# Another order of work inside each segment of a memory-recurrent attention kernel: value projections later, transposes in pairs, softmax in two queue entries

## The chip, the cores and the metric

The kernel runs on one core of a Trainium2 chip. The core has a matrix engine (PE; its weight loads are listed as PEld), a vector engine (DVE), a scalar engine (ACT), a general engine (POOL) and a sync engine (SP), which here only issues transfers. Sixteen DMA engines move data between HBM and the on-chip memory. Each engine takes its own list of instructions strictly in order, and a semaphore wait at the head of a list holds up everything behind it. The metric is the device time in microseconds (us); lower is better.

## The reference, cut to what matters

The sequence of 2048 tokens with 640 features is worked through in 64 segments of 32 tokens. Eight memory rows are carried from one segment to the next, so a segment can't start before the one before it has ended.

```python
for s in range(n_seg):                       # 64, one after the other
    h = concat([mem, x[:, 32*s:32*s+32]])    # 8 memory rows + 32 tokens = 40 rows
    q = einsum('btd,dhe->bhte', h, Wq)       # 32 heads of 192
    k = einsum('btd,dhe->bhte', h, Wk)
    v = einsum('btd,dhe->bhte', h, Wv)
    p = softmax(where(mask, q @ k.T * 192**-0.5, -1e9))
    o = einsum('bhte,hed->btd', p @ v, Wo)
    mem = o[:, :8]                           # into the next segment
    outs.append(o[:, 8:])
b   = (gelu(x @ w_gate) * (x @ w_up)) @ w_down
g   = sigmoid((x * gate_w).sum(-1, keepdims=True))
out = g * concat(outs) + (1 - g) * b
```

## The kernel before, in words

A first stage computes the whole feed-forward branch `b` and stores it in HBM. A second stage (the left stage, lines 795 to 823) computes the projections of Q and K for those eight tokens of each segment whose values don't depend on the memory, for all segments at once, and stores them in HBM ("left stores", four DMAs for each group of heads, issued by ACT). The third stage is the chain of 64 segments, and it takes most of the time. Four segments make a group of 128 rows; in the text q0 to q3 are the first to the fourth segment of such a group. A q0 segment does twice the matmuls in its value projections, since it also does the memory-free rows of V for the whole group (`left` in `v_oct`), and it finishes the output of the previous group (`out_group`, `out_store`).

Inside a segment the 32 heads are taken as four octets of eight heads, numbered 0 to 3. `PROG` (line 464) is the order of the work, written out by hand: a list of items such as `("q", 1)`. `segment` (line 1025) walks through it and hands each operation to `_Sched.add`, which appends it to its engine's list and finds out which earlier operations it has to wait for. So the order of `PROG` is the order of every engine's queue.

- `q` and `k` (`cmode`, L871): the projection of one octet, five weight pieces with four matmuls each, into one bank of PSUM. Then `rows_evac` (ACT, L877) copies the bank to the row buffer `rows_sb` in on-chip memory. There is one such buffer, so the copy for K is queued behind the transposes of Q.
- `tq` and `tk` (`row_transp`): three PE transposes (L883) of the row buffer, and the evacuation into `Qs` on DVE (L887) or into `Ks` on ACT (L890, L894).
- `v` (`v_oct`, L905): as `q`, evacuated by ACT (L916) into one of two buffers; in q0 a second bank is evacuated by DVE (L919).
- `sc` (`scores`): a mask matmul (L926) and 16 score matmuls (L937) into bank 5 or 6 (octet even or odd), then the whole softmax: maximum (L952) and subtraction (L954) on DVE, exponential on ACT (L956), sum (L958), reciprocal (L960) and two products (L962, L963) on DVE. It also queues the POOL copies of the left columns for the next octet (L835, L839).
- `pt` (`p_transp`): two PE transposes of the probabilities (L971, L972) into the same bank 5 or 6, spread by two DVE products (L974, L977) into `PTm` and `PTl`.
- `pv` (`pv_oct`): six matmuls (L991, L993) and the evacuation into `uT` by ACT (L1001) and DVE (L1005, L1007).
- `wo` (`wo_part`, L1020): the output projection of an octet in six pieces of ten matmuls each, summed in bank 7 over the whole segment. For octet 2 it is split into three parts. At the end ACT (L1070) writes the memory rows of the next segment.

All other banks come in turn from `misc_bank` (five banks).

Not all weights fit in on-chip memory. The planner (lines 480 to 509) adds up the `COST` entries along `PROG` for a due time of every weight piece, and picks the pieces to be streamed so that they are evenly spaced in time, as many as memory needs: 24 of the 84 pieces. The others stay resident. A streamed piece goes through a ring of five slots: SP issues the DMA for a piece (L549) as soon as the piece that was five places earlier has been read by PE. In the first segment SP also loads 22 resident pieces (`load_late`, L597) whose memory the left stage held until then, each some 24 pieces ahead of its use and in one queue with the ring.

## Time and profile before

| what | value |
|---|---|
| median of 3 runs | 2227.48 us (2223.69 to 2227.95) |
| the profiled execution | span 2220.5 us; 7.0 us less than the median run, as the span goes from the first instruction to the last only; the page gives no other time of it |
| PE busy | 1912.3 us (86%) |
| DVE, ACT, POOL busy | 943.6 (42%), 799.7 (36%), 273.6 us (12%) |
| moved by DMA | 642.75 MB, 601.01 MB of it by SP's queue |
| left stage ends, chain begins | about 292 us |
| first segment ends | 353.7 us |
| last segment begins | 2185.9 us |

A line such as "L871 PE MATMUL ps<-arena ... x9762 | 465.2, 330 | 61.6 <-DMA ... 20.0" says: 9,762 matmuls from line 871 kept PE busy for 465.2 us, 330 ns each by the record (they overlap); before them PE was idle for 61.6 us in all, 20.0 of it until a DMA landed. "arena" is the on-chip memory and "ps" the PSUM. A row of the view by windows gives a stretch, its length, the busy time of each engine with the number of instructions, the granted clock of TensorE (1.00 is full), the share of time for which the DMA engines were busy, and GB/s. This share can be over 1 for a short window, as packets overlap.

### The profile page before, as it was taken

Reading aid. Unit: us, or ns where it says so; the run is one execution under the profiler, and the core shown is the slowest. Engines: PE = TensorE matmul, PEld = TensorE weight load, DVE = VectorE, ACT = ScalarE, POOL = GpSimd, SP = SyncE. Lnnn points to the kernel's source line nnn. Section 1 sums busy time; section 2 is a strip of 40 time slices with the busy share of each in tenths; the row PEclk is TensorE's granted clock in tenths of the full one; section 3 lists DMA queues with packets and bytes.
Section 4 is the critical chain, followed back from the end, with each engine's and each line's share of the span. In section 5 each row is a group of like instructions: output and inputs, shape, how many; then the busy total and the mean of one; then the engine's idle time right before and its main releaser. Section 6 shows DMA issues by size and latency. Waiting matters only on the chain.

```text
span 2220.5 us, 94985 instructions
## 1 busy us (share of the span) xinstructions
PE 1912.3 (86%) x41834; PEld 1231.3 (55%) x41862; DVE 943.6 (42%) x3184; ACT 799.7 (36%) x2248; POOL 273.6 (12%) x1210
## 2 busy tenths in 40 slices
PE   7999958888888888888888888888888888888887
PEld 3544425555555555555565655555555655555655
DVE  2222223444444444444444444444444544444444
ACT  2222223334333333343333333333333334333333
POOL 0000001111111111111111111111111111111111
PEclk9999989999999999999999999999999999999999
DMA  9203579999999999999999999999999999999998
GB/s 370 88 13 112 150 236 331 322 303 316 301 318 307 324 303 311 305 316 312 319 320 311 316 300 320 306 313 310 320 302 321 309 322 311 315 315 316 310 309 278
DMA packets 363257, 642.75 MB, mean 289 GB/s; under 512 B 60498, under 2 KB 231770, under 8 KB 362842
## 3 DMA queue, kind: packets, MB, share of 16 engines
q1 hardware_dynamic: 311770, 601.01, 80.2%
q10 hardware_dynamic: 51072, 35.66, 5.4%
q8 instruction: 327, 5.36, 0.9%
q14 instruction: 88, 0.72, 0.1%
HBM read 618.74 MB, written 17.83 MB: 287 GB/s over the span
## 4 chain that ended last, share of the span: by engine, by line
PE 46%; DMA 32%; DVE 14%; ACT 3%; issue 3%; ACTq 2%; SPq 0%; DVEq 0%
PE ps L871 12%; DMA arena<-in_A_Wv_dram 10%; DMA arena<-in_A_Wo_dram 9%; PE ps L1020 9%; DMA arena<-in_A_Wk_dram 8%; PE ps L905 7%; DMA arena<-in_A_Wq_dram 4%; DVE arena L974 4%; PE ps L804 3%; PE ps L883 2%; PE ps L742 2%; PE ps L739 2%; ACTq L819 2%; PE ps L757 2%; DVE ps L954 2%
## 5 line engine op out<-in xcount | busy, mean ns | idle before, releaser
L871 PE MATMUL ps<-arena 128*32 128x384 bf16 x10240 | 488.1, 330 | 69.6 <-DMA arena<-in_A_Wk_dram 23.6
L1020 PE MATMUL ps<-arena 128*128 128x40 bf16 x15360 | 457.9, 180 | 64.8 <-DVE arena L1007 38.1
L1020 PEld LDWEIGHTS ps<-arena 128*128 128x128 bf16 x15360 | 428.9, 96 | 88.8 <-DVE arena L1007 49.5
L871 PEld LDWEIGHTS ps<-arena 128*32 128x32 bf16 x10240 | 247.1, 97 | 254.6 <-DMA arena<-in_A_Wk_dram 63.2
L905 PE MATMUL ps<-arena 128*32 128x384 bf16 x6400 | 324.4, 331 | 53.3 <-DMA arena<-in_A_Wv_dram 30.2
L877 ACT ACTIVATE arena<-ps 128x384 bf16<-128x384 f32 x512 | 249.8, 488 | 181.0 <-PE ps L871 105.1
L974 DVE TENSOR_TENSOR arena<-ps,arena 128x320 bf16<-128x320 bf16 x256 | 125.8, 491 | 387.0 <-PE ps L972 387.0
L835 POOL COPY arena<-arena 128x96 bf16<-128x96 bf16 x256 | 67.4, 263 | 1665.0 <-PE ps L937 1138.3
L956 ACT ACTIVATE ps<-ps 104x160 f32<-104x160 f32 x256 | 71.9, 281 | 494.5 <-DVE ps L954 494.5
L905 PEld LDWEIGHTS ps<-arena 128*32 128x32 bf16 x6400 | 144.6, 96 | 175.5 <-DMA arena<-in_A_Wv_dram 59.2
L883 PE MATMUL ps<-arena 128*128 128x128 bf16 x1536 | 175.9, 223 | 32.0 <-ACT arena L877 31.9
L1001 ACT ACTIVATE arena<-ps 128x320 bf16<-128x320 f32 x256 | 112.3, 439 | 215.4 <-PE ps L993 213.8
L991 PE MATMUL ps<-arena 128*128 128x160 bf16 (+1 forms) x768 | 130.5, 260 | 57.1 <-DVE arena L977 39.6
L916 ACT ACTIVATE arena<-ps 128x384 bf16<-128x384 f32 x256 | 125.6, 491 | 139.0 <-PE ps L905 138.7
L839 POOL COPY arena<-arena 64x32 bf16<-64x32 bf16 (+1 forms) x768 | 165.4, 215 | 47.3
L883 PEld LDWEIGHTS ps<-arena 128*128 128x128 bf16 x1536 | 88.1, 98 | 135.7 <-ACT arena L877 91.1
L952 DVE TENSOR_REDUCE arena<-ps 104x4 f32<-104x160 f32 x256 | 80.9, 316 | 149.3 <-PE ps L937 149.3
L894 ACT ACTIVATE arena<-ps 64x128 bf16<-64x128 bf16 x512 | 136.8, 267 | 6.3
L887 DVE COPY arena<-ps 128x384 bf16<-128x384 bf16 x256 | 89.4, 349 | 102.0 <-PE ps L883 102.0
L993 PE MATMUL ps<-arena 128*128 128x64 bf16 (+1 forms) x768 | 124.5, 202 | 4.0 <-ACT arena L877 4.0
L958 DVE TENSOR_REDUCE arena<-ps 104x4 f32<-104x160 f32 x256 | 83.1, 325 | 99.8 <-ACT ps L956 99.8
L991 PEld LDWEIGHTS ps<-arena 128*128 128x128 bf16 x768 | 72.3, 97 | 91.2 <-DVE arena L977 90.7
(81 smaller groups left out, 1886.3 us busy)
## 6 DMA issues: line engine op xcount, KB each, us to landing
arena<-in_A_Wo_dram SPq DMA_DIRECT2D x591, 320.0 KB, 4.7
arena<-in_A_Wv_dram SPq DMA_DIRECT2D x398, 384.0 KB, 5.2
arena<-in_A_Wk_dram SPq DMA_DIRECT2D x340, 384.0 KB, 5.3
arena<-in_A_Wq_dram SPq DMA_DIRECT2D x276, 384.0 KB, 5.0
left_qk_scratch<-arena ACTq DMA_DIRECT2D x16, 768.0 KB, 8.7
arena<-left_qk_scratch ACTq DMA_DIRECT2D x64, 192.0 KB, 4.6
arena<-in_A_x_dram SPq DMA_DIRECT2D x4, 640.0 KB, 15.0
ffn_b_scratch<-arena ACTq DMA_DIRECT2D x16, 160.0 KB, 1.8
```

The source lines that it names most:

```text
L839: S_.add("pool", lambda e, a=a, b=b, lo=lo, hi=hi, sa=sa: e.tensor_copy(out=Ks[lo:hi, a:b, L:R], in_=stg[lo:hi, o, 1, sa:sa + b - a]), rea ...
L871: S_.add("pe", [lambda e, j=j, k=k, g_=g_: e.matmul(ps[32 * j:32 * j + 32, bank, 0:384], Hb[hb][:, k, 0:L], g_[:, 384 * j:384 * (j + 1)], ...
L877: S_.add("act", lambda e: e.activation(out=rows_sb, in_=ps[:, bank, 0:384], func=ACTF.Copy), reads=[r_ps[bank]], writes=[r_rows], name="ro ...
L883: S_.add("pe", [lambda e, c=c: e.transpose(pv[:, c * 128:(c + 1) * 128], rows_sb[:, c * 128:(c + 1) * 128], ident) for c in range(3)], rea ...
L894: S_.add("act", lambda e, a=a, lo=lo: e.activation(out=Ks[lo:lo + 64, a:a + 4, 0:L], in_=src[lo:lo + 64, 1], func=ACTF.Copy), reads=[r_ps[ ...
L905: return [lambda e, j=j: e.matmul(ps[32 * j:32 * j + 32, bk, 0:384], lhs, g_[:, 384 * j:384 * (j + 1)], start=(k == 0), stop=(k == KT - 1) ...
L916: S_.add("act", lambda e: e.activation(out=v_sb[o % NVB], in_=ps[:, bank, 0:384], func=ACTF.Copy), reads=[r_ps[bank]], writes=[r_v[o % NVB ...
L974: S_.add("dve", lambda e: e.tensor_tensor(out=PTm, in0=apx(pv[:, 512:616], [[64, 2], [0, 4], [1, R]]), in1=apx(mbd, [[0, 2], [1, 4], [0, R]]),
L991: return [lambda e: e.matmul(full, v[:, e0:e0 + 128], PTm[:, ia:ib], start=True, stop=False, skip_group_check=True), lambda e: e.matmul(pa ...
L993: lambda e: e.matmul(part, vl[:, e0:e0 + 128], PTl[:, ia:ib], start=False, stop=True, skip_group_check=True)]
L1001: S_.add("act", lambda e: e.activation(out=apx(u[:, 0, 0, :], [[2 * R, 2], [3 * R, 4], [1, R]]), in_=ps[:, A, 0:2 * W].rearrange("p (c t r ...
L1020: fns.append(lambda e, g_=g_, i=i, c=c, n=n, tl=tl, cc=cc, u=u: e.matmul(ps[:, OB, n * R:(n + 1) * R], g_[:, i, n * 128:(n + 1) * 128], u[ ...
```

## The change

The operations of a segment are the same, and their numbers too; the order in which the queues get them is another.

- `PROG` is rewritten. The value projections stand before the transposes (octets 0 and 1), or far behind (`v` 2 behind `pt` 1, `v` 3 behind `pt` 3); `tq` and `tk` always follow each other; `pt` and `pv` of an octet have other work between them.
- There are two row buffers, one for Q and one for K. `rows_evac` for K is queued directly behind its projection.
- `scores` ends with the subtraction. Exponential, sum, reciprocal and products are a function of their own, `probs`, queued by a new item `sm`.
- The extra work that hung on `k` (output of the previous group, transposes of x, copies, gate) now hangs on `tk`.
- The second row buffer takes 768 bytes of each partition from the resident weights, and the `COST` entries are others (`sc` 0.5, `pv` 0.45, `wo` 0.26, `tq` and `tk` 0.25, `sm` 0).

```diff
-    wsB["rows"] = al(768)
+    wsB["rows"] = al(2 * 768)
...
-    PROG = [("q", 0), ("k", 0), ("tq", 0), ("v", 0), ("tk", 0),
-            ("q", 1), ("k", 1), ("sc", 0), ("tq", 1), ("v", 1), ("tk", 1),
-            ("q", 2), ("k", 2), ("pt", 0), ("sc", 1), ("tq", 2), ("pv", 0), ("v", 2), ("tk", 2),
-            ("q", 3), ("k", 3), ("pt", 1), ("sc", 2), ("tq", 3), ("pv", 1), ("v", 3), ("tk", 3),
-            ("wo", 0), ("pt", 2), ("sc", 3), ("pv", 2), ("wo", 1), ("wo", 2, 0), ("pt", 3), ("wo", 2, 1), ("pv", 3),
-            ("wo", 2, 2), ("wo", 3)]
+    PROG = [("q", 0), ("k", 0), ("v", 0), ("tq", 0), ("tk", 0),
+            ("q", 1), ("k", 1), ("v", 1), ("sc", 0), ("tq", 1), ("tk", 1), ("sm", 0),
+            ("q", 2), ("k", 2), ("sc", 1), ("tq", 2), ("tk", 2), ("pt", 0), ("sm", 1),
+            ("q", 3), ("k", 3), ("sc", 2), ("pv", 0), ("tq", 3), ("tk", 3), ("pt", 1), ("sm", 2),
+            ("v", 2), ("sc", 3), ("wo", 0), ("pv", 1), ("pt", 2), ("sm", 3),
+            ("wo", 1), ("pv", 2), ("pt", 3), ("v", 3),
+            ("wo", 2, 0), ("wo", 2, 1), ("pv", 3), ("wo", 2, 2), ("wo", 3)]
...
-    COST = dict(q=0.17, k=0.17, v=0.2, sc=0.6, pt=0.2, pv=0.5, wo=0.27, tq=0.2, tk=0.2)
+    COST = dict(q=0.17, k=0.17, v=0.2, sc=0.5, sm=0.0, pt=0.2, pv=0.45, wo=0.26, tq=0.25, tk=0.25)
...
-    def rows_evac(bank):
-        S_.add("act", lambda e: e.activation(out=rows_sb, in_=ps[:, bank, 0:384], func=ACTF.Copy),
-               reads=[r_ps[bank]], writes=[r_rows], name="rows evac")
+    def rows_evac(m, bank):
+        S_.add("act", lambda e: e.activation(out=rows_sb[m], in_=ps[:, bank, 0:384], func=ACTF.Copy),
+               reads=[r_ps[bank]], writes=[r_rows[m]], name="rows evac")
...
         S_.add("dve", lambda e: e.tensor_tensor(out=S3, in0=S3, in1=mxb, op=ALU.subtract),
                reads=[rb, rst], writes=[rb], name="smax sub")
+
+    def probs(s, o):
...
         S_.add("act", lambda e: e.activation(out=S3, in_=S3, func=ACTF.Exp, bias=0.0, scale=scale),
                reads=[rb], writes=[rb], name="smax exp")
...
             if kind in ("q", "k"):
-                qkbank[kind] = misc_bank()
-                cmode(s, "qk".index(kind), i, qkbank[kind])
-                if kind == "q":
-                    rows_evac(qkbank["q"])
-                if kind == "k" and i == 0 and q == 0 and g > 0:
+                m = "qk".index(kind)
+                bank = misc_bank()
+                cmode(s, m, i, bank)
+                rows_evac(m, bank)
+            elif kind == "tq":
+                row_transp(s, 0, i)
+            elif kind == "tk":
+                row_transp(s, 1, i)
+                if i == 0 and q == 0 and g > 0:
                     out_group(g - 1, misc_bank())
...
-            elif kind == "tq":
-                row_transp(s, 0, i)
-                rows_evac(qkbank["k"])
-            elif kind == "tk":
-                row_transp(s, 1, i)
+            elif kind == "sm":
+                probs(s, i)
```

More of the change, by code (lines that the diff above doesn't have):

```diff
@@ L383, in _build @@
     r_Kz = [sreg(o_K + 8 * R * 2, 4 * R * 2, 64, 128), sreg(o_K + 12 * R * 2, 4 * R * 2, 0, 64)]
-    rows_sb = bview(wsB_off["rows"], 768)
-    r_rows = sreg(wsB_off["rows"], 768)
+    rows_sb = [bview(wsB_off["rows"] + b * 768, 768) for b in range(2)]
+    r_rows = [sreg(wsB_off["rows"] + b * 768, 768) for b in range(2)]
     stg = bview(wsB_off["stg"], NOCT * 2 * LW * 2).rearrange("p (o m c i) -> p o m c i", m=2, c=12, i=M)
@@ L882, in row_transp @@
         pv = psb(bank)
-        S_.add("pe", [lambda e, c=c: e.transpose(pv[:, c * 128:(c + 1) * 128], rows_sb[:, c * 128:(c + 1) * 128], ident)
-                      for c in range(3)], reads=[r_rows, r_ident], writes=[r_ps[bank]], name="T%s s%d o%d" % ("qk"[m], s, o))
+        S_.add("pe", [lambda e, c=c: e.transpose(pv[:, c * 128:(c + 1) * 128], rows_sb[m][:, c * 128:(c + 1) * 128], ident)
+                      for c in range(3)], reads=[r_rows[m], r_ident], writes=[r_ps[bank]], name="T%s s%d o%d" % ("qk"[m], s, o))
         src = pv[:, 0:384].rearrange("p (c t r) -> p c t r", t=4, r=L)
@@ L955, in scores @@
                reads=[rb, rst], writes=[rb], name="smax sub")
+    def probs(s, o):
+        bank = 5 + o % 2
+        S3 = ps[0:104, bank, 0:4 * R].rearrange("p (t r) -> p t r", r=R)
+        mxs, sms, rcs = [x[0:104, :] for x in st_f[o % 2]]
+        rst = r_st[o % 2]
+        rcb = rcs.rearrange("p (t o) -> p t o", o=1).broadcast_to([104, 4, R])
+        rb = r_ps[bank]
         S_.add("act", lambda e: e.activation(out=S3, in_=S3, func=ACTF.Exp, bias=0.0, scale=scale),
@@ L1026, in segment @@
         g, q = s // 4, s % 4
-        qkbank = {}
         for item in PROG:
@@ L1043, in segment @@
                         x_group_transposes(g + 1, misc_bank())
-                if kind == "k" and i == 2:
+                if i == 2:
                     if s + 1 < NSEG:
```

3 lines of the change are left out of this document (1 added, 2 removed).

## The prediction

> **What bounds the kernel now.** I read the page first, then the view by windows, then groups and waits of PE.
>
> ```profile
> span 2220.5 us, 94985 instructions
> ```
>
> The page's shares mix three stages over this span. So I cut the chain at the end of each memory copy (L1070) and asked for 61 of its segments: all at once, then each class q0 to q3 in its turn (last row, and the sum over its segments: 15, 15, 16, 15).
>
> ```profile
> 381.62:2185.94 1804.32, 1560.68 (x38513) 1048.73 (x38513) 822.97 (x2911) 690.62 (x2028) 254.44 (x1128) 0.99 0.93 313
> ...
> 1980.25:2010.76 30.51, 27.73 (x693) 18.89 (x693) 15.82 (x52) 11.44 (x33) 4.08 (x18) 1.00 0.90 302
> sum 463.79, PE 417.23 PEld 283.20 DVE 237.54 ACT 171.69 POOL 61.19; mean PE 27.82 PEld 18.88 DVE 15.84 ACT 11.45 POOL 4.08
> ...
> 2010.76:2040.17 29.41, 24.79 (x608) 16.33 (x608) 12.59 (x46) 11.18 (x33) 4.08 (x18) 1.00 0.95 319
> sum 442.70, PE 375.66 PEld 247.90 DVE 188.95 ACT 168.44 POOL 61.18; mean PE 25.04 PEld 16.53 DVE 12.60 ACT 11.23 POOL 4.08
> ...
> 1922.21:1950.86 28.65, 24.47 (x608) 16.50 (x608) 12.60 (x46) 11.17 (x33) 4.08 (x18) 1.00 0.94 321
> sum 453.79, PE 391.00 PEld 263.30 DVE 201.57 ACT 179.00 POOL 65.25; mean PE 24.44 PEld 16.46 DVE 12.60 ACT 11.19 POOL 4.08
> ...
> 1950.86:1980.25 29.39, 24.95 (x618) 16.68 (x618) 12.99 (x47) 11.44 (x34) 4.46 (x20) 1.00 0.96 316
> sum 444.04, PE 376.79 PEld 254.33 DVE 194.92 ACT 171.50 POOL 66.83; mean PE 25.12 PEld 16.96 DVE 12.99 ACT 11.43 POOL 4.46
> ```
>
> The last three columns are the granted clock, the DMA share and GB/s. A q0 segment takes 463.79 / 15 = 30.9 us with PE busy for 27.8 and DMA for 0.90 of it. The others take 29.5, 28.4 and 29.6 us with PE busy for 25.0, 24.4 and 25.1 and DMA at 0.94 to 0.96. The waits of PE in one q0 segment (first fence) and in the q1 after it (second) show why:
>
> ```profile
> PE ps L905 <- ACT arena L877: 0.9, 2, 0.5
> PE ps L1020 <- DVE arena L1007: 0.8, 2, 0.5
> PE ps L991 <- DVE arena L977: 0.7, 2, 0.4
> PE ps L871 <- ACT arena L1070: 0.3, 1, 0.3
> ```
>
> ```profile
> PE ps L1020 <- DMA arena<-in_A_Wo_dram: 0.7, 2, 0.4
> PE ps L871 <- DMA arena<-in_A_Wq_dram: 0.6, 1, 0.6
> PE ps L1020 <- DVE arena L1007: 0.6, 2, 0.4
> PE ps L991 <- DVE arena L977: 0.4, 1, 0.4
> ...
> PE ps L871 <- DMA arena<-in_A_Wk_dram: 0.4, 1, 0.4
> ```
>
> In q0 PE waits for no DMA: PE and its engine waits set the pace. In the others it waits for weights as well. How full the ring is follows from the issues:
>
> ```profile
> arena<-in_A_Wo_dram SPq DMA_DIRECT2D x591, 320.0 KB, 4.7
> arena<-in_A_Wv_dram SPq DMA_DIRECT2D x398, 384.0 KB, 5.2
> arena<-in_A_Wk_dram SPq DMA_DIRECT2D x340, 384.0 KB, 5.3
> arena<-in_A_Wq_dram SPq DMA_DIRECT2D x276, 384.0 KB, 5.0
> ```
>
> A piece is on its way for about 5.0 us, and 24 of them come in 29.6 us, so 4.1 of five slots are in flight on average. The ring can hardly ask for more. **Segments q1 to q3 are bound by the stream, q0 by PE.** This decides what a PE wait is worth: nearly all in q0, little elsewhere.
>
> **The change part by part.** The waits of PE in the same 61 segments:
>
> ```profile
> L1020 PE MATMUL ps<-arena 128*128 128x40 bf16 x14640 | 436.7, 180 | 62.0 <-DVE arena L1007 36.2 <-DMA arena<-in_A_Wo_dram 22.4 <-issue 1.7
> L905 PE MATMUL ps<-arena 128*32 128x384 bf16 x6080 | 305.7, 329 | 49.8 <-DMA arena<-in_A_Wv_dram 27.0 <-ACT arena L877 21.4 <-issue 0.2
> L883 PE MATMUL ps<-arena 128*128 128x128 bf16 x1464 | 167.2, 223 | 11.8 <-ACT arena L877 11.7
> L991 PE MATMUL ps<-arena 128*128 128x160 bf16 x732 | 124.1, 259 | 54.6 <-DVE arena L977 37.8
> L993 PE MATMUL ps<-arena 128*128 128x64 bf16 x732 | 118.5, 202 | 4.0 <-ACT arena L877 4.0
> ```
>
> *Second row buffer, softmax in two parts.* The K copy now follows its own projection, and the exponential is queued behind the K evacuations. Before, the order of ACT put the exponential first:
>
> ```profile
> 1047.01 0.28 ACT L956 ACTIVATE ps<-ps 104x160 f32<-104x160 f32 x1 [1.90 <-DVE ps L954]
> 1047.21 0.48 ACT L877 ACTIVATE arena<-ps 128x384 bf16<-128x384 f32 x1
> ...
> 1047.74 1.65 PE L905 MATMUL ps<-arena 128*32 128x384 bf16 x36 [0.47 <-ACT arena L877]
> ```
>
> The copy stood behind an exponential that waited for DVE, and the value matmuls, which in q0 take K's bank next, waited 0.47 us for it, twice a segment. All waits on L877 go (21.4 + 11.7 + 4.0 = 37.1 us): 0.9 in a q0, and (37.1 - 15 x 0.9) / 46 = 0.5 in another. New: for octets 2 and 3 a score group now stands where a value projection stood. For octet 2 a copy of 0.48 us and its start against `sc` and `tq` leaves about 0.2 us of wait at `tk`; nothing at the lower bound, 0.5 (the whole copy) at the upper.
>
> *`pt` and `pv` apart.* The 54.6 us before L991 go, 0.9 a segment: behind each `pt` there is now a `wo`, or `q`, `k` and `sc`, 1.8 us (436.7 / 244 for a `wo`) and more against the 0.77 us of L974 and L977 together. If DVE were late by more than 1 us, that cover would be gone.
>
> *New waits in the second half.* The two DVE products, and how `wo` follows `pv` now:
>
> ```profile
> L974 DVE TENSOR_TENSOR arena<-ps,arena 128x320 bf16<-128x320 bf16 x256 | 125.8, 491 | 387.0 <-PE ps L972 387.0
> ...
> L977 DVE TENSOR_TENSOR arena<-ps,arena 128x128 bf16<-128x128 bf16 x256 | 71.7, 280 | 0.0
> ...
> 1062.53 0.69 PE L1020 MATMUL ps<-arena 128*128 128x40 bf16 x20
> 1063.46 1.67 PE L1020 MATMUL ps<-arena 128*128 128x40 bf16 x60 [0.24 <-DVE arena L1007]
> ```
>
> Before, 20 matmuls lie between `pv` 3 and the `wo` that reads its result, and 0.24 us are left; the evacuation takes 0.93 us. `wo` 1 now stands behind `pv` 1 with only the two transposes of `pt` 2 between: a wait of about 0.7 us. The one in front of `wo` (2,0), 0.35 on average (36.2 / 61 less 0.24), goes, as `v` 3 and `pt` 3 lie there. So +0.35; the ends are 0 and 0.7. `sc` 3 writes bank 6, which `pt` 1 used just before; only `v` 2 (305.7 / 304 = 1.0 us) covers, while DVE has to finish the maximum of `sc` 2, `uT`, Q and both products. I take 0.4 us in q1 to q3, none in q0 where `v` 2 is twice as long; the ends are 0 and 0.77.
>
> So PE's own need falls by 0.9 + 0.9 - 0.35 - 0.2 = 1.25 us in q0, and by 0.5 + 0.9 - 0.35 - 0.2 - 0.4 = 0.45 in the others.
>
> *What is streamed.* The planner's arithmetic, redone with the new `PROG`, `COST` and 768 bytes less, gives 24 pieces again, but 8 of Wo, 6 of V, 5 of K and 5 of Q where 9, 6, 5 and 4 stood: one piece of 320 KB became one of 384. Its price is 64 KB at the queue's own rate:
>
> ```profile
> q1 hardware_dynamic: 311770, 601.01, 80.2%
> ```
>
> 0.802 x 2220.5 us for 601 MB makes 0.19 us for 64 KB (65,536 bytes). By the landing times it is less: 0.5 us more (4.7 against 5.2) with 4.1 in flight makes 0.12. I take 0.12, since small and large pieces share the same queue and the difference of landing is measured there; at a share of about 0.945 (the rows of q1 to q3 show 0.94 to 0.96) that is 0.13 us a segment where the stream binds. The ends are 0 and 0.2. The spacing is as even as before: with each item at its PE time, five streamed pieces in a row span 4.5 to 6.1 us before and 4.5 to 6.4 after.
>
> *Moved extras, POOL and SP.* `out_group`, the x transposes and the gate move by one value projection and two transposes; their results are needed a segment later. POOL's left copies still have the two projections in front of the next `sc`. All at nothing; POOL is busy for 4.1 of 29.6 us a segment.
>
> *First segment, once.* ACT sits in the issue of the left stores and the load behind them, with Q's copy queued behind:
>
> ```profile
> 313.46 0.50 PE L883 MATMUL ps<-arena 128*128 128x128 bf16 x3 [19.64 <-ACT arena L877]
> ...
> 312.00:316.00 4.00, 2.54 (x31) 1.32 (x35) 0.36 (x1) 0.98 (x2) 0.14 (x1) 0.50 0.87 213
> 316.00:320.00 4.00, 4.00 (x71) 1.81 (x65) 0.56 (x1) 2.16 (x6) 0.77 (x4) 0.68 0.56 165
> ```
>
> Now `v` 0 runs before that wait and frees a slot, so SP gets further down its list of late loads. The idle DMA time of the two windows, 0.13 x 4 + 0.44 x 4 = 2.3 us, is what this can win. I take 2, with ends of -4 and +2. Of the clock the row shows 0.50 after the wait. The Trainium skill (TensorE: Matmul & The Clock Gate, What's actually happening) says that an idle window of about 3.4 us halves the clock; this row agrees, and by that rule `v` 0 in the shadow wins only its full-clock time, as what follows starts cold instead.
>
> *The sum.* In q0 the stream needs 0.90 x 30.9 + 0.12 = 27.9 us, at the share of 0.945 of the others 29.6; PE needs 30.9 - 1.25 = 29.7. Two needs that near to each other are not met in step: I take 29.9, so -1.0 us, 15 times: -15. In the 48 others: +0.13 x 48 = +6.2, and PE, ready 0.45 us earlier, keeps the ring fuller; from a share of 0.945 to 0.948, inside what the rows show, is 0.1 us, so -4.8. The first segment: -2. In all 15.6 less than the profiled execution's span of 2220.5; that span lies 7.0 below the median of the runs, which I keep: 2227.5 - 15.6 = 2212 us.
>
> **The rivals.**
>
> *A: the stream has room.* Then PE's gain counts everywhere: 15 x 1.25 + 46 x 0.45 = 39, so with the first segment 2186. For it: with many transfers waiting the engines do more:
>
> ```profile
> 300.00:304.00 4.00, 0.00 (x0) 0.00 (x0) 0.00 (x0) 0.00 (x0) 0.00 (x0) 0.50 1.05 402
> ```
>
> Against it: there the queue was deep, here it is five slots, 4.1 of them used. The Trainium skill says to judge DMA by HBM use, not by the engines' busy share (Perfetto Trace Analysis, Identifying the Most-Contended Engine), and gives about 358 GB/s a core (DMA: Bandwidth & Descriptors, Specifications); 313 is 87% of it, so by that rule A holds. The 402 GB/s of this row disagree with the limit.
>
> *B: the waits only move.* The new waits stand at their upper ends: `wo` 1 at 0.7, `sc` 3 at 0.77, `tk` at 0.5. In q1 to q3 PE then loses 1.97 - 1.4 = 0.57 us, which fits into its DMA waits (0.7 + 0.6 + 0.4 = 1.7 us in the q1 shown); in q0 1.8 - 1.2 = 0.6 is left, 9 us in all, and the larger piece takes 6.2 of it: about 2225, no change. For it: `pv` 1 and its reader are neighbours now.
>
> *C, slower: the stream binds q0 too.* If its share stays at 0.90 there, with or without PE's waits, only the larger piece is left: 64 x 0.13 to 64 x 0.2 = 8 to 13 us, so 2236 to 2240. It decides once the new DMA waits of PE in a q0 segment pass 1.25 us. For it: a ring of five can't work ahead into q0. Against it: not one DMA wait in the q0 rows above.
>
> **How the numbers follow.** The forecast has 0.48 (its own range 2197 to 2222), A 0.16, B 0.13, C 0.23. Faster, the same, slower: 0.64, 0.13, 0.23; the runs shown lie within 0.2%, which is about what can be told from no change. The range, 2180 to 2237, leaves out the outer part of A and of C.
>
> **What would show it.** Right: no wait on the row copies in q0 segments; those near 29.9 us with DMA waits; q1 to q3 unchanged within 0.3 us with DMA at 0.95; a wait of 0.7 us in front of `wo` 1. Wrong: a DMA share of 0.97 or more with q1 to q3 below 28.7 us (A), or a q0 still near 30.9 us (C).

## The result, and the profile after

The changed kernel takes 2204.35 us (median of 4 runs, 2201.96 to 2208.51); the kernel before takes 2225.64 us beside it (4 runs, 2223.69 to 2227.95). The ratio is 0.9914, with a 95% interval of 0.9894 to 0.9933: 0.9% faster, 21 us by the medians. The profiled execution took 2205.25 us, with a span of 2203.5 us.

The same cut at the memory copies (L1078 now) gives the view by windows of the kernel after: the whole of the 61 segments, then the sums over the 15, 15, 16 and 15 segments of q0 to q3.

```profile
383.10:2168.30 1785.20, 1524.01 (x38513) 1049.37 (x38513) 825.10 (x2911) 734.43 (x2028) 254.50 (x1128) 0.98 0.95 318
...
sum 447.00, PE 402.65 PEld 283.46 DVE 236.65 ACT 180.16 POOL 61.19; mean PE 26.84 PEld 18.90 DVE 15.78 ACT 12.01 POOL 4.08
...
sum 440.00, PE 363.37 PEld 247.01 DVE 190.06 ACT 179.96 POOL 61.20; mean PE 24.22 PEld 16.47 DVE 12.67 ACT 12.00 POOL 4.08
...
sum 452.76, PE 383.06 PEld 260.28 DVE 202.78 ACT 192.79 POOL 65.26; mean PE 23.94 PEld 16.27 DVE 12.67 ACT 12.05 POOL 4.08
...
sum 445.44, PE 374.92 PEld 258.62 DVE 195.60 ACT 181.53 POOL 66.84; mean PE 24.99 PEld 17.24 DVE 13.04 ACT 12.10 POOL 4.46
```

A q0 segment takes 447.00 / 15 = 29.80 us, 1.12 less than before. The 46 others take (440.00 + 452.76 + 445.44) / 46 = 29.09 us on average where they took 29.14. So 16.8 us are gained in q0 and 2.3 in all the other segments of the cut, 19.1 in the whole row. Outside of it 2.1 us are lost (first segment 0.5, second 1.0, end 0.6), and the span is 17.0 us shorter. The DMA share of q0, added up over its 15 windows, rises from 0.90 to 0.94. How far one profile can be trusted in this, a second one of the same kernel shows further down: 30.02 us in q0, 28.82 in the others.

The groups of PE over the same stretch show where its waits went (line numbers are shifted by the diff: L872 is `cmode`, L1028 `wo`, L906 `v`, L884 the Q and K transposes, L999 the first matmuls of `pv`, L927 the mask, L980 the second transpose of `pt`):

```profile
L872 PE MATMUL ps<-arena 128*32 128x384 bf16 x9760 | 477.0, 330 | 96.7 <-DMA arena<-in_A_Wk_dram 55.0 <-DMA arena<-in_A_Wq_dram 19.8 <-ACT arena L1078 17.9
L1028 PE MATMUL ps<-arena 128*128 128x40 bf16 x14650 | 433.1, 181 | 63.6 <-DMA arena<-in_A_Wo_dram 32.8 <-DVE arena L1015 27.3 <-issue 2.4
L906 PE MATMUL ps<-arena 128*32 128x384 bf16 x6080 | 320.6, 332 | 61.6 <-DMA arena<-in_A_Wv_dram 59.8 <-issue 0.3
L884 PE MATMUL ps<-arena 128*128 128x128 bf16 x1464 | 132.3, 221 | 4.2 <-ACT arena L878 3.4
L999 PE MATMUL ps<-arena 128*128 128x160 bf16 x732 | 125.4, 261 | 0.8 <-issue 0.8
...
L927 PE MATMUL ps<-arena 128*40 128x160 bf16 x488 | 61.1, 247 | 8.2 <-DVE arena L985 7.8
...
L980 PE MATMUL ps<-arena 104*128 104x104 bf16 x244 | 52.0, 213 | 26.3 <-DVE arena L1015 20.8 <-ACT arena L1009 5.2
```

The waits on the row copies (37.1 us before) are 3.4, those before `pv` (54.6) are 0.8. The transposes themselves cost less: 132.3 us busy where it was 167.2, for the same 1464. And PE waits for weights much more: 55.0 + 19.8 + 32.8 + 59.8 = 167.4 us, where the classes of the table below add up to 82 us before. Also in a q0 segment there are DMA waits now, in the view of PE's waits of one of them:

```profile
PE ps L872 <- DMA arena<-in_A_Wk_dram: 1.6, 2, 0.9
PE ps L906 <- DMA arena<-in_A_Wv_dram: 0.6, 2, 0.3
...
```

The same reading for every segment, each group's idle time split into what ended it and averaged by class, in us. "PE's need" is the segment less its DMA waits; the lines from the fifth on are kernels of the next section.

| kernel, class | segment | DMA waits of PE | waits on other engines | PE's need |
|---|---|---|---|---|
| before, q0 | 30.92 | 0.19 | 2.57 | 30.73 |
| after, q0 | 29.80 | 1.41 | 1.40 | 28.39 |
| before, q1 / q2 / q3 | 29.51 / 28.36 / 29.60 | 2.17 / 1.44 / 1.59 | 1.85 / 2.06 / 2.47 | 27.3 / 26.9 / 28.0 |
| after, q1 / q2 / q3 | 29.33 / 28.30 / 29.70 | 3.51 / 2.75 / 3.29 | 1.37 / 1.35 / 1.32 | 25.8 / 25.6 / 26.4 |
| after, second profile, q0 | 30.02 | 1.60 | 1.41 | 28.42 |
| after, second profile, q1 / q2 / q3 | 28.53 / 28.47 / 29.50 | 3.23 / 2.88 / 3.23 | 1.26 / 1.36 / 1.34 | 25.3 / 25.6 / 26.3 |
| before + row buffer, q0 | 30.23 | 0.59 | 1.65 | 29.64 |
| before + six slots, q0 | 30.69 | 0.00 | 2.69 | 30.69 |
| after + six slots, q0 | 29.01 | 0.65 | 1.42 | 28.36 |

Without DMA waits PE would do a q0 segment 2.3 us faster than before, and the others 1.3 to 2.0 us faster. Of that 0.9 to 1.1 us were gained in q0, and 0.05 to 0.3 in the others. Waits for weights took the rest. (A wait for an engine that runs out while PE stands for a weight is not in "PE's need". In q0 this hides little: with six slots the DMA waits are half as long, 0.65 us, and the need is the same, 28.36.)

### The profile page after: what moved, and what is told of

It reads as the page before. It is cut to its first block, busy times and chain, and to the rows that moved or that the text cites. A ratio compares the mean times of both kernels' runs of the same rounds, so it can differ in the third digit from the quotient of the medians.

```text
span 2203.5 us, 94933 instructions
## 1 busy us (share of the span) xinstructions
PE 1874.1 (85%) x41862; PEld 1232.9 (56%) x41862; DVE 945.9 (43%) x3184; ACT 845.0 (38%) x2248; POOL 273.6 (12%) x1210
## 4 chain that ended last, share of the span: by engine, by line
DMA 46%; PE 45%; DVE 4%; ACTq 3%; issue 1%; ACT 1%; SPq 0%; DVEq 0%
DMA arena<-in_A_Wv_dram 19%; PE ps L1028 12%; DMA arena<-in_A_Wo_dram 11%; DMA arena<-in_A_Wk_dram 10%; PE ps L872 8%; PE ps L906 7%; DMA arena<-in_A_Wq_dram 5%; PE ps L805 3%; PE ps L743 2%; PE ps L740 2%; ACTq L820 2%; PE ps L758 2%; PE ps L999 2%; PE ps L884 2%; DVE arena L1015 1%
## 5 line engine op out<-in xcount | busy, mean ns | idle before, releaser
L872 PE MATMUL ps<-arena 128*32 128x384 bf16 x10240 | 501.8, 330 | 104.8 <-DMA arena<-in_A_Wk_dram 60.8
L1028 PE MATMUL ps<-arena 128*128 128x40 bf16 x15360 | 454.7, 181 | 68.0 <-DMA arena<-in_A_Wo_dram 36.1
L1028 PEld LDWEIGHTS ps<-arena 128*128 128x128 bf16 x15360 | 420.7, 96 | 109.7 <-DMA arena<-in_A_Wo_dram 42.6
L872 PEld LDWEIGHTS ps<-arena 128*32 128x32 bf16 x10240 | 240.0, 96 | 311.7 <-DMA arena<-in_A_Wk_dram 125.7
L906 PE MATMUL ps<-arena 128*32 128x384 bf16 x6400 | 337.1, 332 | 65.0 <-DMA arena<-in_A_Wv_dram 63.2
L906 PEld LDWEIGHTS ps<-arena 128*32 128x32 bf16 x6400 | 148.6, 97 | 198.2 <-DMA arena<-in_A_Wv_dram 127.2
L1013 DVE CAST arena<-ps 64x160 bf16<-64x160 f32 x256 | 80.4, 314 | 236.8 <-PE ps L1001 236.8
L884 PE MATMUL ps<-arena 128*128 128x128 bf16 x1536 | 139.7, 222 | 27.1 <-ACT arena L878 26.2
L999 PE MATMUL ps<-arena 128*128 128x160 bf16 (+1 forms) x768 | 132.0, 261 | 0.8 <-issue 0.8
L884 PEld LDWEIGHTS ps<-arena 128*128 128x128 bf16 x1536 | 89.8, 98 | 60.5 <-ACT arena L878 39.4
L891 ACT ACTIVATE arena<-ps 128x256 bf16<-128x256 bf16 x256 | 98.1, 383 | 62.1 <-PE ps L884 43.4
```

Source lines behind the costliest of these rows:

```text
L872: S_.add("pe", [lambda e, j=j, k=k, g_=g_: e.matmul(ps[32 * j:32 * j + 32, bank, 0:384], Hb[hb][:, k, 0:L], g_[:, 384 * j:384 * (j + 1)], ...
L884: S_.add("pe", [lambda e, c=c: e.transpose(pv[:, c * 128:(c + 1) * 128], rows_sb[m][:, c * 128:(c + 1) * 128], ident) for c in range(3)], ...
L906: return [lambda e, j=j: e.matmul(ps[32 * j:32 * j + 32, bk, 0:384], lhs, g_[:, 384 * j:384 * (j + 1)], start=(k == 0), stop=(k == KT - 1) ...
L999: return [lambda e: e.matmul(full, v[:, e0:e0 + 128], PTm[:, ia:ib], start=True, stop=False, skip_group_check=True), lambda e: e.matmul(pa ...
L1028: fns.append(lambda e, g_=g_, i=i, c=c, n=n, tl=tl, cc=cc, u=u: e.matmul(ps[:, OB, n * R:(n + 1) * R], g_[:, i, n * 128:(n + 1) * 128], u[ ...
```

## The experiments

Ratios are to the kernel before, run beside each on the same chip.

**The row buffer alone.** The kernel before, with its own order, gets the second buffer, and each copy is queued behind its projection. The planner picks the same 24 pieces.

```diff
-    wsB["rows"] = al(768)
+    wsB["rows"] = al(2 * 768)
...
                 cmode(s, "qk".index(kind), i, qkbank[kind])
-                if kind == "q":
-                    rows_evac(qkbank["q"])
+                rows_evac("qk".index(kind), qkbank[kind])
...
                 row_transp(s, 0, i)
-                rows_evac(qkbank["k"])
```

> The kernel before with the second row buffer and K's copy queued directly behind its projection; old order, softmax in one piece, the same 24 streamed pieces as before. Theory T (q0 is paced by PE, q1 to q3 by the stream): the waits on the row copies go (37.1 us of PE in all), but only q0 gets shorter, by about 0.9 us, so 14 us less than before, and q1 to q3 stay within 0.15 us. Rival A (the stream has room, PE's waits count everywhere): 37 us less than before. If the row buffer is not what pays, less than 5 us.

Measured: 2204.14 us against 2220.15, ratio 0.9935 (0.9912 to 0.9958). The whole chain, q0 and two groups of PE:

```profile
381.75:2168.28 1786.53, 1557.90 (x38513) 1046.49 (x38513) 822.68 (x2911) 709.23 (x2028) 254.40 (x1128) 0.99 0.95 316
...
sum 453.52, PE 413.54 PEld 282.54 DVE 237.36 ACT 176.41 POOL 61.18; mean PE 27.57 PEld 18.84 DVE 15.82 ACT 11.76 POOL 4.08
```

```profile
L883 PE MATMUL ps<-arena 128*128 128x128 bf16 x1464 | 167.2, 223 | 0.3 <-DVE arena L887 0.3
L991 PE MATMUL ps<-arena 128*128 128x160 bf16 x732 | 124.4, 260 | 54.3 <-DVE arena L977 36.8
```

That is 16 us less, as expected for a gain in q0 alone (14), and not the 37 of a stream with room. The row-copy waits are gone, the 54 us before `pv` are all there, and the time is nearly that of the whole change: the intervals of 0.9935 and 0.9914 overlap. In the profile q0 stands at 453.52 / 15 = 30.23 us, between 30.92 and 29.80. So the rest of the reordering takes another 0.43 us out of a q0 in these profiles (0.21 by the second profile of after), and gives nothing that can be told in the others (28.98 us here, 29.09 and 28.82 after).

**What is a wait of PE worth?** Into the kernel before, six more transposes a segment (those of octet 0 done twice), once in q0 only, once in the others only:

```diff
-                      for c in range(3)], reads=[r_rows, r_ident], writes=[r_ps[bank]], name="T%s s%d o%d" % ("qk"[m], s, o))
+                      for c in range(3)] * (2 if o == 0 and s % 4 == 0 else 1), reads=[r_rows, r_ident], writes=[r_ps[bank]], name="T%s s%d o%d" % ("qk"[m], s, o))
```

(`s % 4 != 0` in the second.)

> The kernel before with the six transposes of octet 0 done twice (same result), in q0 segments only: 0.54 us more of PE in 16 segments. Theory T and rival A: q0 grows by 0.5 us, 8.6 us in all. Rival C (the stream paces q0 too): nothing.

> The kernel before with the six transposes of octet 0 done twice in q1 to q3 segments only: 0.54 us more of PE in 48 segments. Theory T: PE's DMA waits there shrink by that, segments grow by at most 0.15 us, 0 to 7 us in all. Rival A: 26 us more.

Measured: in q0 +5.1 us by the medians, 2225.25 against 2220.15, ratio 1.0028 (1.0010 to 1.0047); in the others +3.1 us, 2223.29, ratio 1.0019 (0.9998 to 1.0040). First q0 of the one, then q1 to q3 of the other:

```profile
sum 469.09, PE 421.02 PEld 288.13 DVE 237.36 ACT 172.72 POOL 61.19; mean PE 28.07 PEld 19.21 DVE 15.82 ACT 11.51 POOL 4.08
```

```profile
sum 436.21, PE 375.09 PEld 251.73 DVE 188.92 ACT 169.09 POOL 61.17; mean PE 25.01 PEld 16.78 DVE 12.59 ACT 11.27 POOL 4.08
...
sum 462.95, PE 398.04 PEld 270.52 DVE 201.52 ACT 179.87 POOL 65.27; mean PE 24.88 PEld 16.91 DVE 12.60 ACT 11.24 POOL 4.08
...
sum 447.56, PE 382.16 PEld 258.20 DVE 194.91 ACT 172.31 POOL 66.85; mean PE 25.48 PEld 17.21 DVE 12.99 ACT 11.49 POOL 4.46
```

The added work was half of what the expectations took, 0.54 us: PE is busy for 0.25 us more in a q0 segment of the one (421.02 against 417.23 over 15) and for 0.26 more in the others of the second (1155.29 against 1143.45 over 46). Q0 grew by 31.27 - 30.92 = 0.35 us. The others stand at 1346.72 / 46 = 29.28 against 29.14: 0.14 us, while classes that got no work moved by 0.04 and 0.06 in the same two profiles. By the ratios, 0.0028 x 2220 / 16 = 0.39 us for each of 16 segments against 0.0019 x 2220 / 48 = 0.09 for each of 48, with an interval that reaches from nothing to 0.19. So the same work on PE costs 2.5 (profiles) to 4 times (ratios) as much in a q0 segment as in another: q0 was bound by PE, the others mostly not. If PE's time counted everywhere (rival A), 0.26 us in each of 48 segments would be 12 us, and the interval ends at 9.

**The changed kernel again, and what the stream is made of.** The first run repeats it. In the two others the streamed pieces are chosen by hand, spread over the order (0, 1, 2 for Q, K, V with octet and piece, 3 for Wo; the first kernel's list is shown): 23 instead of 24 (6 of Wo), and 24 with one small piece for a large one (9 of Wo, 64 KB less a segment).

```diff
+    STREAM = [(0, 0, 3), (1, 0, 4), (2, 0, 4), (0, 1, 2), (1, 1, 3), (2, 1, 3), (0, 2, 0), (0, 2, 4), (1, 2, 4), (0, 3, 0), (1, 3, 0), (1, 3, 4), (2, 2, 0), (2, 2, 2), (3, 2), (3, 5), (3, 8), (2, 3, 0), (2, 3, 2), (2, 3, 4), (3, 16), (3, 19), (3, 22)]
+    streamed = {order.index(k) for k in STREAM}
+    nstream = len(STREAM)
```

> The changed kernel again, beside the others on one chip: 0.991 of the kernel before. If the second row buffer alone gives nearly all of the gain (as the run of it suggests), the rest of the change is worth less than 0.2% either way, and this stands within 5 us of that kernel's ratio of 0.9935.

> The changed kernel with the streamed pieces written out by hand: 23 (6 of Wo, 7 of V, 5 of K, 5 of Q) instead of 24 (8, 6, 5, 5), as the memory allows it: 256 KB less a segment, 0.78 us at the queue's own rate. Theory T (the stream binds q1 to q3 and, once PE's waits are gone, q0 nearly too): 0.5 to 0.8 us a segment, 35 to 50 us less than the changed kernel. Rival D (a segment is bound by the time from a freed slot to the landing, or by PE, and not by the amount that is moved): less than 8 us.

> The changed kernel with the mixture of streamed pieces of the kernel before: 9 of Wo and 4 of Q instead of 8 and 5, 64 KB less a segment. Theory T: 0.12 to 0.2 us a segment, 8 to 13 us less than the changed kernel. Rival D: no difference. An uneven spacing would take some of it back.

Measured: 2197.74 us, ratio 0.9890 (0.9850 to 0.9930), for the repetition. By the ratios that is 10 us below the row buffer alone, twice what was allowed for if the rest of the change were worth nothing, but the intervals overlap. With 23 pieces 2165.66 us, 0.9759 (0.9719 to 0.9798): 32 us less, just short of the 35 to 50 expected. With the smaller piece 2200.39 us, 0.9904 (0.9863 to 0.9945): none of the 8 to 13 us that were expected is to be seen, though the interval of 9 us to each side would hide a gain of 6. The chain and the four sums, of the repetition first, then with 23 pieces:

```profile
385.10:2161.31 1776.21, 1516.30 (x38513) 1045.37 (x38513) 825.10 (x2911) 735.60 (x2028) 256.20 (x1128) 0.99 0.95 320
...
sum 450.28, PE 403.13 PEld 284.29 DVE 236.55 ACT 180.33 POOL 61.57; mean PE 26.88 PEld 18.95 DVE 15.77 ACT 12.02 POOL 4.10
...
sum 427.96, PE 358.08 PEld 243.36 DVE 189.92 ACT 180.32 POOL 61.61; mean PE 23.87 PEld 16.22 DVE 12.66 ACT 12.02 POOL 4.11
...
sum 455.51, PE 383.53 PEld 259.77 DVE 202.96 ACT 193.07 POOL 65.72; mean PE 23.97 PEld 16.24 DVE 12.69 ACT 12.07 POOL 4.11
...
sum 442.46, PE 371.57 PEld 257.95 DVE 195.66 ACT 181.88 POOL 67.30; mean PE 24.77 PEld 17.20 DVE 13.04 ACT 12.13 POOL 4.49
```

```profile
381.99:2128.59 1746.60, 1514.66 (x38513) 1047.69 (x38513) 825.51 (x2911) 735.67 (x2028) 256.20 (x1128) 0.99 0.94 316
...
sum 445.60, PE 401.62 PEld 284.23 DVE 236.63 ACT 180.43 POOL 61.59; mean PE 26.77 PEld 18.95 DVE 15.78 ACT 12.03 POOL 4.11
...
sum 429.22, PE 361.68 PEld 246.35 DVE 190.52 ACT 180.57 POOL 61.60; mean PE 24.11 PEld 16.42 DVE 12.70 ACT 12.04 POOL 4.11
...
sum 441.22, PE 380.79 PEld 260.39 DVE 202.93 ACT 193.05 POOL 65.71; mean PE 23.80 PEld 16.27 DVE 12.68 ACT 12.07 POOL 4.11
...
sum 430.56, PE 370.58 PEld 256.72 DVE 195.42 ACT 181.63 POOL 67.30; mean PE 24.71 PEld 17.11 DVE 13.03 ACT 12.11 POOL 4.49
```

Q0 falls from 30.02 to 29.71 us, the others from 28.82 to 28.28. The kernel with 23 pieces streams 256 KB less a segment (8 Wo and 16 others against 6 and 17), so it does not tell pieces from bytes by itself, but the slots fit: 24 pieces through five slots in 1776.21 / 61 = 29.12 us make 6.1 us from issue to issue of one slot, 23 in 28.63 make 6.2. A kernel with more slots and more bytes tells them apart.

**One more slot.** The changed kernel with six slots and 24 pieces, only 6 of them of Wo, so 128 KB more are streamed in each segment; and the kernel before with six slots, 24 pieces with 8 of Wo. Both lists are chosen by hand again, as a sixth slot takes 3,072 bytes of a partition from the resident weights.

```diff
-    B_RING = int(opts.get("ring", 5))
+    B_RING = int(opts.get("ring", 6))
```

> The changed kernel with six ring slots; the sixth takes its room from the residents, so the 24 streamed pieces are 6 of Wo and 18 others, 128 KB more a segment. If the number of transfers in flight limits the stream (4.1 of 5 slots used): the DMA share of q1 to q3 goes from 0.95 to 0.98 or more, and segments get 0.3 us or more shorter, 15 to 30 us less than the changed kernel. If the amount that is moved is the limit at a share near 0.96: 0.2 to 0.4 us longer, 10 to 25 us more.

> The kernel before with six ring slots and nothing else of the change: old order, one row buffer, softmax in one piece; 24 streamed pieces (8 of Wo, 16 others, the same amount as the changed kernel moves, by hand, evenly spaced for the old order). Theory T (each class of segment is bound by the slower of PE's own need and the stream): q0 stays at 30.7 to 30.9 us, as PE paces it; q1 to q3 fall to 27.9 to 28.3 on average, between PE's own need of 27.3 and the stream; 60 to 75 us less than before. Then the change is worth 30 us or more with six slots, against 20 with five. Rival (the ring is all, the change is worth nothing beside it): within 10 us of the changed kernel with six slots (0.9545).

Measured: the changed kernel with six slots 2117.88 us against 2219.45, ratio 0.9545 (0.9516 to 0.9574), faster than both kernels. The kernel before with six slots 2177.63 us against 2222.44, ratio 0.9803 (0.9752 to 0.9853). The chain and the four sums of the first, its issues over the whole span, then the chain and q0 of the second:

```profile
379.48:2091.22 1711.74, 1505.85 (x38513) 1055.77 (x38513) 823.45 (x2911) 733.12 (x2028) 254.48 (x1128) 0.99 0.97 337
...
sum 435.10, PE 399.37 PEld 285.99 DVE 236.29 ACT 180.05 POOL 61.18; mean PE 26.62 PEld 19.07 DVE 15.75 ACT 12.00 POOL 4.08
...
sum 418.46, PE 359.99 PEld 248.96 DVE 189.82 ACT 179.69 POOL 61.18; mean PE 24.00 PEld 16.60 DVE 12.65 ACT 11.98 POOL 4.08
...
sum 432.17, PE 378.79 PEld 263.24 DVE 202.43 ACT 192.84 POOL 65.26; mean PE 23.67 PEld 16.45 DVE 12.65 ACT 12.05 POOL 4.08
...
sum 426.01, PE 367.69 PEld 257.58 DVE 194.91 ACT 180.53 POOL 66.85; mean PE 24.51 PEld 17.17 DVE 12.99 ACT 12.04 POOL 4.46
```

```profile
arena<-in_A_Wv_dram SPq DMA_DIRECT2D x524, 384.0 KB, 6.0
arena<-in_A_Wq_dram SPq DMA_DIRECT2D x340, 384.0 KB, 5.4
arena<-in_A_Wk_dram SPq DMA_DIRECT2D x340, 384.0 KB, 5.6
arena<-in_A_Wo_dram SPq DMA_DIRECT2D x402, 320.0 KB, 5.5
```

```profile
380.84:2145.15 1764.31, 1550.77 (x38513) 1045.62 (x38513) 822.99 (x2911) 692.65 (x2028) 255.97 (x1128) 0.99 0.95 322
...
sum 460.32, PE 415.11 PEld 283.62 DVE 237.49 ACT 171.89 POOL 61.55; mean PE 27.67 PEld 18.91 DVE 15.83 ACT 11.46 POOL 4.10
```

The changed kernel moves more bytes in less time: 337 GB/s where five slots gave 318 and 320, at a share of 0.97. By the ratios that is 77 to 82 us less than with five slots, where 15 to 30 were expected. A piece lands in about 5.6 us, 24 of them in 28.06 us, so 4.8 of six are in flight. The list made by hand and its mixture (6 of Wo) are not the cause: the kernel with 23 pieces has both, with five slots, and moves 316 GB/s. The kernel before gains only in q1 to q3 (29.14 to 28.35 us); its q0 stays at 460.32 / 15 = 30.69, and in the table above it waits for no DMA at all. It gains 45 us, less than the 60 to 75 expected; q1 to q3 stop just above the 27.9 to 28.3 that were given for them. Here the two orders differ by 0.9545 / 0.9803 = 0.974, so the order that was worth 0.9% with five slots is worth 2.6% with six (two chips, and 128 KB a segment to the disadvantage of the better one). Of the difference, q0 has 30.69 - 29.01 = 1.68 us a segment and the others have 28.35 - 27.75 = 0.60. Which part of the change gives it, no run with six slots tells.

**The old order with 23 pieces.** The kernel with the row buffer alone, and 23 pieces chosen by hand for its order:

```diff
+    STREAM = [(0, 0, 3), (1, 0, 3), (2, 0, 1), (0, 1, 0), (1, 1, 0), (1, 1, 4), (2, 1, 1), (0, 2, 0), (1, 2, 0), (1, 2, 4), (2, 2, 0), (2, 2, 3), (0, 3, 1), (1, 3, 1), (1, 3, 4), (2, 3, 0), (2, 3, 4), (3, 3), (3, 6), (3, 10), (3, 15), (3, 18), (3, 23)]
```

> The old order with the second row buffer alone, and 23 streamed pieces of the same bytes as in the changed kernel with 23 (6 of Wo, 17 others, written out by hand, evenly spaced for the old order). Theory T: the stream still binds q1 to q3, so the rest of the new order is worth nothing there, and this kernel stands within 8 us of the changed one with 23 pieces (0.976 of the kernel before). Rival E (a lighter stream lets the rest of the new order pay): 12 us or more above it.

Measured: 2272.39 us against 2219.45, ratio 1.0252 (1.0227 to 1.0276): slower, with 11.6 MB less to move (589.41 MB on SP's queue against 601.01). The chain:

```profile
387.60:2233.95 1846.35, 1578.08 (x38513) 1037.46 (x38513) 822.79 (x2911) 709.19 (x2028) 254.45 (x1128) 0.99 0.91 299
```

By the ratios this is some 110 us above the new order with 23 pieces, where theory T allowed 8. Rival E (12 or more) fits the number but not by its reason, as the stream did not get lighter: the share falls to 0.91 and the rate to 299 GB/s. The pieces were placed unevenly: by the planner's costs 0.92 apart on average up to `wo` and 1.48 between the six pieces of `wo`. PE's waits over the chain show what that does (L875 is `cmode`, L1024 `wo`):

```profile
PE ps L875 <- DMA arena<-in_A_Wk_dram: 67.6, 123, 1.9
...
PE ps L1024 <- DMA arena<-in_A_Wo_dram: 0.4, 1, 0.4
```

In `wo` PE hardly ever waits for a weight, before it all the more (19.2 us for Wk with the planner's 24 pieces in the row-buffer kernel). Cut into eighths, a segment has a DMA share of 0.83 in its first and 0.78 in its last eighth, without any DMA wait, and 0.92 to 0.97 in between, where all of the 2.1 us of DMA waits lie. So the stream is left idle at the ends and is behind in the middle. The spacing was not changed by itself, and so this run says nothing on what the order is worth with fewer pieces.

**The changed kernel with one row buffer.** The new order, but K's copy waits behind the transposes of Q again:

```diff
+    rows_sb = [bview(wsB_off["rows"], 768)] * 2
+    r_rows = [sreg(wsB_off["rows"], 768)] * 2
...
-                rows_evac(m, bank)
+                if m == 0:
+                    rows_evac(m, bank)
+                else:
+                    kbank = bank
             elif kind == "tq":
                 row_transp(s, 0, i)
+                rows_evac(1, kbank)
```

> The changed kernel with one row buffer: K's copy is queued behind the transposes of Q again, and nothing stands between these and the transposes of K. PE then waits for a copy of 0.49 us and its start, about 0.75 us, four times a segment. Theory T: q0 grows by the whole 3 us, q1 to q3 by 1 to 1.5 us as their DMA waits take the rest; about 100 us more than the changed kernel. Rival A: 190 us more. If the copies were not what PE waited for: nothing.

Measured: 2259.01 us against 2219.45, ratio 1.0177 (1.0155 to 1.0198), some 60 us more than the changed kernel. From the view of PE's waits over the chain, and the sum of q0:

```profile
PE ps L884 <- ACT arena L878: 159.5, 269, 0.9
```

```profile
sum 466.79, PE 405.20 PEld 285.56 DVE 239.86 ACT 180.62 POOL 61.17; mean PE 27.01 PEld 19.04 DVE 15.99 ACT 12.04 POOL 4.08
```

With `tq` and `tk` next to each other there is nothing to cover the copy, and the wait stands 269 times, 159.5 us. A q0 is 1.1 to 1.3 us longer than in the two profiles of the changed kernel, the others, at 29.86 us, 0.8 to 1.0: the two parts of the change need each other. The expectation of 3 us for q0 failed. PE's own need there grows by 2.6 us, from 28.39 to 30.97 as the table reads it, but its DMA waits fall from 1.41 to 0.15: the stream hides half, since a q0 segment of the changed kernel already waits for weights. The transposes of this kernel serve further down:

```profile
L884 PE MATMUL ps<-arena 128*128 128x128 bf16 x1464 | 166.0, 222 | 159.8 <-ACT arena L878 159.5
```

**The softmax.** In one kernel all of it is queued at `sc`; in the other only the exponential is moved there.

```diff
             elif kind == "sm":
-                probs(s, i)
+                pass
             elif kind == "sc":
                 scores(s, i)
+                probs(s, i)
```

```diff
                reads=[rb, rst], writes=[rb], name="smax sub")
+        S_.add("act", lambda e: e.activation(out=S3, in_=S3, func=ACTF.Exp, bias=0.0, scale=scale),
+               reads=[rb], writes=[rb], name="smax exp")
```

> The changed kernel with the softmax queued in one piece again, directly behind its scores. DVE then does sum, reciprocal and products of octet 2 (about 1 us, behind a wait for the exponential) before the evacuations that score group 3 waits for, so its wait grows by about 1 us where the value projection in front of it is short (q1 to q3), less in q0. Theory T: hidden in part by DMA waits, 5 to 20 us more than the changed kernel. Rival A: about 60 us more. If the split is idle: no difference.

> The changed kernel with the exponential queued in the scores item again; sum, reciprocal and products stay where they are. ACT's evacuations of K stand behind an exponential that waits for DVE again, but no value projection stands behind these any more. Theory T: within 5 us of the changed kernel. If the place of the exponential in ACT's queue is what pays: 10 us or more above it.

Measured: the whole softmax early 2307.23 us against 2220.15, ratio 1.0403 (1.0369 to 1.0437); the exponential early 2196.87 us against 2223.84, ratio 0.9878 (0.9841 to 0.9915), the same as the changed kernel beside it. The first is no plain undoing: there is one buffer of probabilities, and `sc` of the next octet now stands ahead of `pt`, so octets 0 to 2 use the next octet's probabilities and `pt` has to wait for a softmax that has only begun. From PE's waits between 1000 and 1400 us (L971 is the last product of the softmax, L979 the first transpose of `pt`):

```profile
PE ps L979 <- DVE arena L971: 37.4, 34, 1.6
```

About 2.8 us in each segment, a wait that its expectation (5 to 20 us in all) had not seen. So this run doesn't price the split: the split is there so that the new order works with one buffer. Where the exponential stands among ACT's copies makes no difference that can be told.

## Why the prediction was right, and where only by luck

**The frame held.** "Segments q1 to q3 are bound by the stream, q0 by PE": q1 to q3 moved by 0.05 us of their 29 (0.3 in the second profile), q0 by 1.12 (0.9); the doubled transposes and the kernel before with six slots show the same from the other side. For q0 29.9 us was predicted, 29.80 came (30.02 in the second profile).

**But PE's saving was sized too small, and this cancelled against the stream.** The step "PE's own need falls by 1.25 us in q0, by 0.45 in the others" failed: it fell by 2.3, and by 1.3 to 2.0. The waits on engines went as computed in q0 (2.57 to 1.40, that is 1.17). What was left out is busy time: 27.82 us in a q0 segment before, 26.84 after, 0.98 less. Of that the transposes have 0.57 (34.9 us over 61 segments). Three transposes took 167.2 / 488 = 0.34 us before, six in a row take 132.3 / 244 = 0.54: a second set that follows at once costs far less than one that starts anew. The kernel with only the row buffer keeps 167.2; and in the new order with one row buffer, where the copy parts the two sets again, they take 166.0. So it is their standing next to each other that saves it. The other 0.4 us of busy time was not traced to lines, and 0.2 us are pauses too short to be listed as waits.

The stream's side was right: "at the share of 0.945 the stream needs 29.6 in q0" against 29.80, with a share of 0.94 and DMA waits of 1.41 us. What was too small is what the sum added since the two needs "are not met in step": 0.2 us on PE's 29.7, where 1.4 stand on 28.39. The kernel with the row buffer alone shows what the saving that I had would have brought: it needs 29.64, nearly the 29.7 of the sum, and takes 30.23, since 0.59 us of DMA waits come on top. That is a gain of 0.7 us in q0 and not the 1.0 of the sum. So the number was met because a saving taken too small and a wait taken too small cancelled; that part is luck. Rival C put its point of decision at 1.25 us of new DMA waits in a q0 segment; there are 1.2, and 1.4 in the second profile. It did not come about because PE's saving was nearly twice the 1.25 that this point was reckoned from.

**Terms one by one.** The row copies: 37.1 us foreseen to go, 33.7 went; by the run with the row buffer alone this makes most of the gain. The wait before `pv`: 54.6 foreseen, 53.8 went; what that is worth by itself no run shows. `wo` 1 was to cost a net 0.35 us a segment; `wo` and the second transpose of `pt` 2, where the wait now shows, have 27.3 + 26.3 = 53.6 us in the rows of L1028 and L980 against 36.2, so 0.29. `sc` 3 was sized 0.4 and is 8.2 / 46 = 0.18; `tk` 2 was sized 0.2 and is 4.2 / 61 = 0.07. So rival B did not come about.

**The larger piece, +6.2 us, stays unproven.** Six slots move 128 KB a segment more and are faster, so the bytes alone do not set the pace of this stream. What the larger piece costs with five slots is not settled: with 64 KB less q1 to q3 take 1329.91 / 46 = 28.91 us against 28.82, but the interval of the time is too wide for 6 us. The sum had 1.4 us for q1 to q3 in all, and -2.3 came (-15 in the second profile).

**"The ring can hardly ask for more" was true of the slots, and I read it as true of the stream.** The prediction took 4.1 of five slots in flight as the ring being full, and then priced bytes. The runs show a limit by the slots: the sixth takes the same order from 318 to 337 GB/s with more bytes to move. Five slots are not slow while all of them are in use: in a row further down, where PE stands still and five pieces are in flight, they move 381 GB/s for 1 us. So what spoke for rival A, the 402 GB/s with a deep queue, was a sound sign of room, which this kernel could not reach with five slots; its condition, q1 to q3 below 28.7 us at a share of 0.97, is just what six slots show (27.75 us, 0.97). The Trainium skill (Perfetto Trace Analysis, Roofline) adds that 358 GB/s is the share of a core whose neighbour is busy too, and that one core alone can draw more, up to about 435 GB/s by its DMA engines; the 402 and 337 GB/s agree with that, and the prediction's remark that 402 disagrees with the limit left this condition out.

**The first segment** was to win 2 us and lost 0.5. The two windows and the first work after them, in the kernel after:

```profile
312.00:316.00 4.00, 0.00 (x0) 0.00 (x0) 0.00 (x0) 0.13 (x1) 0.00 (x0) 0.50 1.07 267
316.00:320.00 4.00, 3.58 (x42) 1.86 (x46) 0.36 (x1) 2.43 (x7) 0.86 (x4) 0.50 0.53 106
...
316.42 0.88 PE L884 MATMUL ps<-arena 128*128 128x128 bf16 x6 [21.88 <-ACT arena L878]
```

The DMA engines are indeed busy in the first window (1.07 instead of 0.87), but PE comes back 3 us later, after 21.88 us instead of 19.64. ACT's copies stand behind its issue of the four left stores and one load. By the order of time, SP's earlier loads share the engines with these stores; no run tried it apart.

**The size.** 15.6 us were predicted, 21.3 came by the medians, and 17.0 between the profiled spans; the span before lies 5.1 below its median, the one after 0.9. The prediction carried the 7.0 us between span and median over as if it came from how a span is taken. In all executions on record that have both, the time is only 1.7 to 2.9 us above the span. So 4 to 5 of the 7.0 were the scatter of runs, and this is about what the gain by the medians has above that of the spans.

## What to carry to other kernels

Sort a loop's iterations by what they do and ask in each class how much of PE's waiting is for DMA: here a wait taken from PE paid where that was near zero, and showed up elsewhere mostly as a wait for weights. Before bytes are counted, compare the transfers in flight with the slots of the ring: if nearly all slots are in flight and the rate is below what a deep queue reached, one more slot can be worth more than a better order (2.0% against 0.9% here, each by itself, and 4.5% together). Look also at where in an iteration the streamed pieces stand: with 23 of them bunched before `wo` the stream idled in one part of the segment and held PE up in another. Count what neighbours on PE save in busy time too: a second set of transposes behind the first cost 0.20 us here where one by itself cost 0.34.

## What the hardware showed that I had not expected

**Waits for weights can cost clock as well.** The mean granted clock fell from 0.986 to 0.979 by the view by cores, while PE's waits for weights doubled. One of the two longest segments after (34.0 us; none before is over 31.5) shows how, in windows of 1 us:

```profile
1935.00:1936.00 1.00, 0.00 (x0) 0.00 (x0) 0.00 (x0) 0.00 (x0) 0.00 (x0) 1.00 1.01 381
...
1937.00:1938.00 1.00, 0.69 (x20) 0.44 (x20) 0.00 (x0) 0.13 (x1) 0.00 (x0) 1.00 0.48 191
1938.00:1939.00 1.00, 1.00 (x16) 0.14 (x8) 0.00 (x0) 0.36 (x1) 0.00 (x0) 0.65 0.27 71
1939.00:1940.00 1.00, 1.00 (x27) 0.90 (x24) 0.30 (x1) 0.49 (x1) 0.26 (x1) 0.50 0.84 273
1940.00:1941.00 1.00, 1.00 (x13) 0.80 (x15) 0.64 (x4) 0.54 (x2) 0.65 (x3) 0.50 0.94 221
1941.00:1942.00 1.00, 1.00 (x20) 0.49 (x16) 0.78 (x2) 0.55 (x2) 0.00 (x0) 0.65 0.71 268
```

PE stands still for a weight piece for 2.5 us, resumes at 1937.31, and a microsecond later its clock is at 0.50, by the four rows for about 3.4 us. While PE stands it frees no slot: by the timeline SP issues nothing between 1934.08 and 1937.70. PE waits for weights twice more in this segment, for 0.9 us at 1948.6 and for 2.4 us at 1952.0; whether the first stall or the lost clock brought these on is not shown. Nor is why the DMA share falls to 0.27 at 1938, as four or five pieces are still in flight there by their times of landing. The Trainium skill (TensorE: Matmul & The Clock Gate, What's actually happening) gives an idle window of about 3.4 us as what throttles the clock; here a single wait of 2.5 us, with one of 1.1 us shortly before, came before the half clock. Why such a stall came in these segments and not in others stays open.

**Issuing can hold an engine for long.** In the timeline of ACT before, the four left stores take 17.15 us at the issue alone, and everything behind them waits:

```profile
292.80 17.15 ACTq L819 DMA_DIRECT2D left_qk_scratch<-arena  x4
```

After, it is 20.94 us.
